# Attention and a three-stage mixer on one core: the third batch's k^T v and attention recorded earlier, the fourth batch's k, v and q asked for later

## The chip, the cores and the metric

The kernel runs on one core of one Trainium2 chip. The metric is device time in microseconds (us), the median of several executions. Engines are named as in the profile: PE is TensorE's matmul, PEld its weight load, DVE is VectorE, ACT is ScalarE, POOL is GpSimd, SP is SyncE. SP computes nothing here: it issues most of the DMAs, one after the other, and an instruction of SP that waits holds up every DMA behind it.

## The reference

For each of 8 batches (8 heads, 576 positions, head size 64, model size 512), in float32:

```python
kv  = einsum('bhsd,bhse->bhde', k, v)            # k^T v, 64 x 64 per head
out = einsum('bhsd,bhde->bhse', q, kv)
out = out / sqrt(mean(out * out, -1) + 1e-6) * g_norm
x   = out, heads side by side                    # (8, 576, 512)

theta = x @ w_theta                              # mixer, stage 1
y = w_tok_r @ (x * cos(theta)) + w_tok_i @ (x * sin(theta))
u = x + y
x = u + relu(u @ w_ch)

h = relu(x^T @ w_tok1) @ w_tok2                  # stage 2, over positions
u = x + h^T
return u + relu(u @ w_ch1) @ w_ch2               # stage 3, over channels
```

## The kernel before

Batches are numbered 0 to 7, so the third is batch 2 and the fourth is batch 3. A name in a row such as `xt24` is tile xt of batch 2, position tile 4. The 576 positions are cut into four tiles of 128 and a last one of 64, which is tile 4.

Float32 factors are split into a high and a low float16 part, so a product is three matmuls (helper `mm3`, lines 105 to 107). One batch passes through these units:

- `kv(o, part)`, unit K: k^T v into the PSUM tile kvp. Part 0 takes k and v tiles 0 and 1, part 1 takes 2, 3 and 4 (the last two have 96 rows each). Then ACT and DVE copy kvp into `kvbd` (lines 414, 415). There are three buffers each for k and v, so tiles 3 and 4 are asked for only when part 0 has read tiles 0 and 1.
- `attend(o, r)`, "a" and "n" in the recording tables: tile r of q times kvbd into PSUM (po, line 429); ACT squares (442), DVE sums (444), POOL takes a power (445, 446), DVE scales (x, 449); ACT and DVE split x into xs (465, 467); SP has a DMA transpose it into xt (468).
- `rotate(o, r)`, "r": theta = x @ w_theta (pt; line 105, or 532 for batch 0), then sine and cosine on ACT and DVE (541 to 560; 581 to 618 for tile 4) into zh and zl. Tile 4 ends with a DMA transpose from zt to zh (623).
- `residual(o, r)`, "s": x, turned, into R.
- `mix`, unit M (py), and for batch 1 `outer` (pa, pb): the two w_tok products. `channel`, unit C (pr): u @ w_ch, evicted by DVE (716), split (717, 724) and turned by a DMA transpose (728) in pairs. `token1`, unit H (ph), and `token2`, unit T (pu, evicted at 759): stage 2.
- Spare units "w" (`stash`): weights of stage 3 are loaded (wa_r), worked over on ACT, DVE and POOL (160 to 170, 335 to 345) and stored (wad), one batch of them beside each batch of the main work.

PE, DVE, ACT, POOL and SP each take their instructions in a fixed order. It comes from the order in which the code records the units, from `placed`, `lead` and `keep_in_program_order`, which tie instructions of one engine in the order of recording, and from a scheduler that orders the rest when the program is built. A recorded unit runs in steps: each next unit advances all that are pending.

`run(units, o, nxt, after, also)` records units of one batch; `also` says what is recorded beside each of them, for batch `nxt` (a, r, s) or batch `after` (n and unit K). `load_heads(b)` asks for k and v tiles 0 to 2 and for q of batch b. There is one q buffer, so q of batch 3 can only be asked for when batch 2's last attend tile has been read.

The change lies where batch 1 is in the main loop (`b == 1`), with batch 0's units H and T left over from before and batch 2's front work recorded beside them. Of what stands there before, the tables say:

```python
run(["K00"] + TOKEN1 + ["K10"] + TOKEN2, before, None, nxt, {"T00": "n0", "T02": "n1", "T10": "n2 w", "T12": "n3"})
run(CHANNEL[:1], o, nxt, None, {"C00": "a4 l"})
```

Batch 2's K units stand on both sides of batch 0's unit H, its x tiles 0 to 3 beside batch 0's unit T, its x tile 4 and the loads of batch 3 ("l") beside the first unit C of batch 1, and batch 3's K units in the middle of batch 1's units C and H.

Of the kernel before, what the change touches and what calls it, by code (L numbers as in the profile page):

```python
# [28 lines left out]
def attn_mixer_kernel(  # L29
# [175 lines left out]
    def theta_split(j):  # L205

        hi = stg.tile([P, 2 * DM], F16, tag="val", name=f"wt{j}h", bufs=2)[:, :DM]
        nc.scalar.activation(hi, wt[:, j], AF.Copy, scale=gt)
        yield
        nc.vector.scalar_tensor_tensor(wtl[:, j], wt[:, j], gt, hi, ALU.mult, ALU.subtract)  # L210
        yield
        nc.scalar.activation(wth[:, j], hi, AF.Copy)
# [138 lines left out]
    def stash_wide(g, k):  # L351
        return stash(w_ch1, f"wa{g}{k}_", k * P, g * P, [t[:, g, k] for t in wad])

    def stash_narrow(g, m):
        return stash(w_ch2, f"wb{g}{m}_", g * P, m * P, [t[:, g, m] for t in wbd])
# [12 lines left out]
    def load_kv(o, r):  # L368
        b, n = o.b, ROWS[r + 1] - ROWS[r]

        pool, bufs = (kp, 2) if b < 2 and r > 2 else (fp, 3)
        for t, src in (("k", k), ("v", v)):
            dst = pool.tile([P, DM], F32, tag=t, name=f"{t}{b}{r}", bufs=bufs)[:n]
            ins = nc.sync.dma_start(dst, src[b, ROWS[r]:ROWS[r + 1], :])
            if b == 2 and r < 3:
                tc.keep_in_program_order(ins)
            o.kv.append(dst)

    def load_heads(b):
        o = Batch()  # L380
        o.b, o.zh = b, None
        o.kv = []
        for r in range(NR + 1 if b < 2 else 3):
            load_kv(o, r)
        o.q = fp.tile([P, HP, SM + P], F32, tag="q", name=f"q{b}", bufs=1)
        qs = qT[b].rearrange("h p s -> p h s")
        if b == 0:
            nc.sync.dma_start(o.q[:, :, :P], qs[:, :, :P])
        else:
            load_q(o, 0)  # L390
        return o

    def load_q(o, at):
        qs = qT[o.b].rearrange("h p s -> p h s")
        for dst, src in ((slice(at, S), slice(at, S)), (slice(S, None), slice(SM, S))):
            ins = nc.sync.dma_start(o.q[:, :, dst], qs[:, :, src])
            if o.b == 2:
                tc.keep_in_program_order(ins)

    def kv(o, part):  # L400
# [546 lines left out]
    def go(unit, lead=False):  # L947
        advance()
        next(unit)
        (leading if lead else pending).append(unit)  # L950

    def advance():

        for units in (leading, pending):
            for g in list(units):
                try:
                    next(g)
                except StopIteration:
                    units.remove(g)

    def flush():
        while pending or leading:
            advance()
# [3 lines left out]
    def spare(n=1):  # L967
        for _ in range(min(n, len(extra))):
            go(extra.pop(0))

    def front(unit, o, r):
        if o is not None:
            go(unit(o, r))

    tk, cp, first = [], [], iter(())
    for j in range(KD):
        if j == KD - 1:
            o = load_heads(0)
        go(theta_weight(j))
# [6 lines left out]
    nxt = load_heads(1)  # L986
# [18 lines left out]
    MIX, CHANNEL, TOKEN2 = ([f"{k}{c}{i}" for c in range(2) for i in range(KD)] for k in "MCT")  # L1005
    TOKEN1 = [f"H{c}{i}" for c in range(2) for i in range(KJ)]
    UNITS = {"M": mix, "C": channel, "H": token1, "T": token2}

    def run(units, o, nxt, after, also):

        for u in units:
            kind, c, i = u[0], int(u[1]), int(u[2])
            if kind == "K":
                front(kv, after, c)
            else:
                go(UNITS[kind](o, c, i), True)
            for what in also.get(u, "").split():
                if what == "w":
                    spare()
                elif what == "l":  # L1020
                    if o.b + 2 < B:
                        loaded.append(load_heads(o.b + 2))
                elif what[0] == "a":
                    front(attend, nxt, int(what[1]))
                elif what[0] == "n":
                    front(attend, after, int(what[1]))
                elif what[0] == "r":
                    front(rotate, nxt, int(what[1]))
                elif what[0] == "s":
                    front(residual, nxt, int(what[1]))  # L1030
                elif what == "f":
                    next(first, None)
# [3 lines left out]
    STEADY = MIX[:6] + CHANNEL[:2] + MIX[6:] + CHANNEL[2:4] + ["K00"] + CHANNEL[4:] + TOKENS1[1:] + TOKEN2  # L1036
# [4 lines left out]
    for b in range(B):  # L1041
        loaded.clear()
        if b == 0:
            splits = [theta_split(j) for j in range(KD)]
            for what in "t t t t M2 r0 M3 r1 r4 . l X0 r2 X1 . r3 w X4 w w X2 w s0 s1 s2 s3 X3 .".split():
                if what == ".":
                    advance()
                elif what == "t":
                    go(splits.pop(0))
                elif what == "w":  # L1050
                    spare()
                elif what == "l":
                    loaded.append(load_heads(2))
                elif what[0] == "M":
                    go(mix(o, 1, int(what[1])), True)
                else:
                    go({"r": rotate, "X": outer, "s": residual}[what[0]](nxt, int(what[1])))
            spare(len(extra))
            flush()
            start_ctx.close()  # L1060
            wp.append(stash_ctx.enter_context(tc.tile_pool(name="wp", bufs=2, side="right", reuse_waits="tile")))
            tk.append(tok_ctx.enter_context(tc.tile_pool(name="tk", bufs=1, side="left", reuse_waits="tile")))
            extra += token_weights()
            spare(3)
            advance()
            run(CHANNEL, o, nxt, None, {"C00": "w", "C02": "w"})
            after = loaded[0]
            spare(len(extra))
            extra += [stash_wide(g, k) for g in range(KH) for k in range(DH)]
            extra += [stash_narrow(g, m) for g in range(KH) for m in range(MH)]  # L1070
            before = o
        elif b == 1:
            go(mixed(o))
            run(MIX[6:], o, nxt, None, {})
            run(["K00"] + TOKEN1 + ["K10"] + TOKEN2, before, None, nxt, {"T00": "n0", "T02": "n1", "T10": "n2 w", "T12": "n3"})
            run(CHANNEL[:1], o, nxt, None, {"C00": "a4 l"})
            after = loaded[0]
            run([u for u in STEADY[STEADY.index("C01"):] if u[0] != "M"], o, nxt, after, {
                "C01": "r0", "C02": "r1", "C10": "r2 w", "C11": "r4 s0", "C12": "s1", "H00": "s2", "H01": "r3 w s3", "H11": "n0", "T01": "n1 w", "T12": "w",
            })  # L1080
        elif b + 2 < B:
            at = STEADY.index("M02") + 1
            run(STEADY[:at], o, nxt, None, BESIDE)
            after = loaded[0]
            run(STEADY[at:], o, nxt, after, BESIDE)
        elif b + 2 == B:
            run(MIX[:6] + CHANNEL[:2] + MIX[6:] + CHANNEL[2:], o, nxt, None, {
                "M00": "a2 w", "M01": "a3", "M02": "a4 r0", "M03": "r1", "M10": "r2", "M11": "r3", "C00": "w", "M12": "r4",
            })

            spare(len(extra))
            flush()
            before, after = o, None
            stash_ctx.close()
            front_ctx.close()
            cw = ctx.enter_context(tc.tile_pool(name="cw", bufs=1, side="right", reuse_waits="tile"))
            wa = pair([P, KH, DH, 7, P], "wa", cw)
            for g in range(KH):
                for i in range(2):
                    nc.sync.dma_start(wa[i][:, g], wad[i][:, g])  # L1100
            first = chunks(0)
            ck = next(first)
        else:
            run(MIX[:6], o, None, None, {"M00": "f", "M01": "f", "M02": "f", "M03": "f"})
            run(TOKEN1, before, None, None, {})
            run(CHANNEL[:2] + MIX[6:], o, None, None, {})
            run(TOKEN2[:4], before, None, None, {})
            run(CHANNEL[2:] + TOKEN1[:2], o, None, None, {})
            run(TOKEN2[4:], before, None, None, {})
            run(TOKEN1[2:] + TOKEN2, o, None, None, {})  # L1110
        o, nxt = nxt, after
# [52 lines left out]
```

## Time and profile before

| | us |
|---|---|
| median of 3 runs | 1094.99 |
| lowest and highest run | 1094.35, 1098.6 |
| the profiled execution, its device time | 1095.65 |
| its span, first to last instruction | 1093.6 |
| PE busy in the span | 1064.7 (97%) |
| DVE busy | 807.4 (74%) |
| ACT busy | 564.9 (52%) |
| POOL busy | 184.4 (17%) |

The span is the time between the first and the last instruction of the profiled execution; its device time is 2.05 us longer. Times in rows are counted from the start of the span. Idle time of an engine that nobody waits for costs nothing.

### The profile page before, as it was taken

To read this page: it belongs to the slowest core of one execution; us is meant where nothing else is said; L and a number is where in the kernel's file an instruction comes from. 1 tells how busy PE (TensorE), PEld (TensorE's weight loads), DVE (VectorE), ACT (ScalarE), POOL (GpSimd) and SP (SyncE) were. 2 spreads that over 40 slices of the span, in tenths; PEclk is the share of its full clock that TensorE was granted. 3 is DMA by queue.
4 is the path that set the end of the run, shared out by engine and by line. 5 is a ranking of instruction groups with operands and counts; after the bars stand their busy time and mean duration, and the time that the engine had idled before them with its cause. 6 is when DMAs were issued, how large, how long until landed. Compare 5 with 4: busy or idle time off the path is not lost.

```text
span 1093.6 us, 21467 instructions
## 1 busy us (share of the span) xinstructions
PE 1064.7 (97%) x8856; PEld 812.1 (74%) x8856; DVE 807.4 (74%) x1430; ACT 564.9 (52%) x950; POOL 184.4 (17%) x255
## 2 busy tenths in 40 slices
PE   4999998999999999999999999999999999999998
PEld 3676775876768667776876777777777777777776
DVE  3999977887888878987564775858486775758484
ACT  2877547465565554656331645445363644446360
POOL 2331041533614526252000000000000000000000
DMA  9918378738858487452547301020201102020101
GB/s 304 295 21 228 71 211 194 230 81 242 205 118 241 117 222 203 119 163 51 150 169 228 124 28 60 12 77 7 82 1 44 45 23 66 12 77 1 45 1 44
DMA packets 145122, 126.05 MB, mean 115 GB/s; under 512 B 91968, under 2 KB 121792, under 8 KB 145024
## 3 DMA queue, kind: packets, MB, share of 16 engines
q1 hardware_dynamic: 139584, 104.23, 35.2%
q0 software_dynamic: 5440, 20.45, 5.2%
q8 instruction: 69, 1.13, 0.5%
q14 instruction: 29, 0.24, 0.1%
HBM read 74.25 MB, written 29.88 MB: 95 GB/s over the span
## 4 chain that ended last, share of the span: by engine, by line
PE 72%; DVE 11%; DMA 8%; ACT 4%; SPq 2%; POOL 2%; issue 1%; ACTq 0%; DVEq 0%; POOLq 0%
PE pa L105 5%; PE pa L107 5%; PE pa L106 5%; PE na L105 4%; PE na L107 4%; PE na L106 4%; DMA xt<-xs 3%; PE py L105 3%; PE py L106 3%; PE py L107 3%; PE pc L107 2%; PE pc L106 2%; PE pc L105 2%; PE nc L105 2%; PE nc L106 2%; PE nc L107 2%
## 5 line engine op out<-in xcount | busy, mean ns | idle before, releaser
L105 PE MATMUL py<-wmh,zh 128*128 128x320 f16 (+1 forms) x468 | 134.2, 287 | 1.1 <-DVE x L449 0.8
L106 PE MATMUL py<-wml,zh 128*128 128x320 f16 (+1 forms) x468 | 134.2, 287 | 0.0
L107 PE MATMUL py<-wmh,zl 128*128 128x320 f16 (+1 forms) x416 | 119.3, 287 | 0.0
L107 PE MATMUL na<-gh,wbl 128*128 128x288 f16 x384 | 109.3, 286 | 0.0
L106 PE MATMUL pa<-o,wah 128*128 128x288 f16 x384 | 109.2, 286 | 0.0
L106 PE MATMUL na<-gl,wbh 128*128 128x288 f16 x384 | 109.1, 286 | 0.0
L105 PE MATMUL pa<-o,wah 128*128 128x288 f16 x384 | 108.4, 286 | 0.0
L107 PE MATMUL pa<-o,wal 128*128 128x288 f16 x384 | 107.8, 286 | 0.0
L105 PE MATMUL na<-gh,wbh 128*128 128x288 f16 x384 | 106.0, 286 | 0.2
L832 DVE TENSOR_TENSOR gl<-sum,gh 128x1152 f16<-128x1152 f32 x48 | 65.0, 1354 | 21.9 <-ACT gh L831 21.9
L106 PEld LDWEIGHTS <-wbh 128*128 128x128 f16 x672 | 65.7, 98 | 17.8 <-issue 1.0
L105 PEld LDWEIGHTS <-wah 128*128 128x128 f16 x672 | 65.8, 98 | 16.6
L107 PEld LDWEIGHTS <-wal 128*128 128x128 f16 x672 | 65.8, 98 | 16.6
L106 PEld LDWEIGHTS <-wah 128*128 128x128 f16 x672 | 65.8, 98 | 16.6
L107 PEld LDWEIGHTS <-wbl 128*128 128x128 f16 x672 | 65.7, 98 | 16.6
L105 PEld LDWEIGHTS <-wbh 128*128 128x128 f16 x672 | 65.7, 98 | 16.6
L106 PE MATMUL pr<-ul,wch 128*128 128x256 f16 (+1 forms) x256 | 73.0, 286 | 0.0
L105 PE MATMUL pr<-uh,wch 128*128 128x256 f16 (+1 forms) x256 | 72.9, 286 | 0.0
L107 PE MATMUL pr<-uh,wcl 128*128 128x256 f16 (+1 forms) x256 | 72.6, 286 | 0.0
L105 PEld LDWEIGHTS <-zh 128*128 128x128 f16 x576 | 56.4, 98 | 17.8 <-ACT zh L557 1.2
L831 ACT ACTIVATE gh<-sum 128x1152 f16<-128x1152 f32 x48 | 55.5, 1157 | 25.6 <-DVE sum L879 25.6
L446 POOL TENSOR_TENSOR ri<-ss,mhalf 128x8 f32<-128x8 f32 x40 | 68.1, 1702 | 2.6
(293 smaller groups left out, 2915.6 us busy)
## 6 DMA issues: line engine op xcount, KB each, us to landing
c<-u2d SPq DMA_DIRECT2D x32, 288.0 KB, 4.3
out<-c SPq DMA_DIRECT2D x64, 144.0 KB, 1.8
q<-in_q SPq DMA_DIRECT2D x7, 1152.0 KB, 6.1
k<-in_k SPq DMA_DIRECT2D x24, 256.0 KB, 5.1
v<-in_v SPq DMA_DIRECT2D x24, 256.0 KB, 5.3
wa_r<-in_w_ch SPq DMA_DIRECT2D x24, 256.0 KB, 4.4
wb_r<-in_w_ch SPq DMA_DIRECT2D x24, 256.0 KB, 4.6
wad<-wa POOLq DMA_DIRECT2D x24, 224.0 KB, 4.1
```

What stands on the lines that cost most here:

```text
L105: nc.tensor.matmul(acc, ah, bh, start=first and i == 0, stop=False, **more)
L106: nc.tensor.matmul(acc, ah, bl, start=False, stop=False, **more)
L107: nc.tensor.matmul(acc, al, bh, start=False, stop=last and i == n - 1, **more)
L446: nc.gpsimd.tensor_tensor(ri, ss, mhalf, ALU.pow)
L831: nc.scalar.activation(h.hi[:, 3:], h.s, AF.Copy)
L832: nc.vector.tensor_tensor(h.lo[:, 3:], h.s, h.hi[:, 3:], ALU.subtract)
```

## The change

At the end of batch 0's part, both K units of batch 2 are recorded among batch 0's units C. Batch 2's x tiles 0 to 3 are recorded beside the last M unit and batch 0's H and T units, tile 4 ("a4") beside C01 instead of C00. Batch 3's k and v are asked for ("l") at C11, in a fixed order on SP, and its q apart from them ("q") at H10. Batch 3's K units stand between and behind batch 1's units H, and its first attend tiles later in unit T.

```diff
-            if b == 2 and r < 3:
+            if b == 2 and r < 3 or b == 3:
                 tc.keep_in_program_order(ins)
...
         if b == 0:
             nc.sync.dma_start(o.q[:, :, :P], qs[:, :, :P])
-        else:
+        elif b != 3:
             load_q(o, 0)
...
-            if o.b == 2:
+            if o.b in (2, 3):
                 tc.keep_in_program_order(ins)
...
+                elif what == "q":
+                    load_q(after, 0)
...
-            run(CHANNEL, o, nxt, None, {"C00": "w", "C02": "w"})
             after = loaded[0]
+            run(CHANNEL[:4] + ["K00"] + CHANNEL[4:7] + ["K10"] + CHANNEL[7:], o, nxt, after, {"C00": "w", "C02": "w"})
...
             go(mixed(o))
-            run(MIX[6:], o, nxt, None, {})
-            run(["K00"] + TOKEN1 + ["K10"] + TOKEN2, before, None, nxt, {"T00": "n0", "T02": "n1", "T10": "n2 w", "T12": "n3"})
-            run(CHANNEL[:1], o, nxt, None, {"C00": "a4 l"})
+            run(MIX[6:], o, nxt, None, {"M13": "a0"})
+            run(TOKEN1 + TOKEN2, before, nxt, None, {"H01": "a1", "H11": "a2", "T01": "a3", "T10": "w", "T11": "r0"})
+            run(CHANNEL[:1], o, nxt, None, {"C00": "r1"})
+            run(CHANNEL[1:6], o, nxt, None, {"C01": "a4 r2", "C10": "w", "C11": "s0 l"})
             after = loaded[0]
-            run([u for u in STEADY[STEADY.index("C01"):] if u[0] != "M"], o, nxt, after, {
-                "C01": "r0", "C02": "r1", "C10": "r2 w", "C11": "r4 s0", "C12": "s1", "H00": "s2", "H01": "r3 w s3", "H11": "n0", "T01": "n1 w", "T12": "w",
+            run(CHANNEL[6:] + ["H00", "H01", "K00", "H10", "H11", "K10"] + TOKEN2, o, nxt, after, {
+                "C12": "r4 s1", "H00": "s2", "H01": "r3 w s3", "H10": "q", "T10": "n0", "T11": "w", "T12": "n1 w",
             })
```

What this makes of the engines' orders is shown at two places.

The first place is x tile 4 of batch 2, while batch 1's units C are on PE (pr102 is unit C02, pr110 to pr113 are C10 to C13). On DVE, before, from the eviction of pr102 to xs24, the last step before tile 4 is turned:

```order
L716 SCALAR_TENSOR_TENSOR R1_608<-pr102_1836,R1_608 128x256
L545 SCALAR_TENSOR_TENSOR cs20_1825<-cs20_1825,pt20_1812 128x512
L449 TENSOR_TENSOR x24_1765<-po24_1757,ri24_1763 128x512
L724 SCALAR_TENSOR_TENSOR xs102_1835<-R1_608,xs102_1835 128x256
L716 SCALAR_TENSOR_TENSOR R1_608<-pr103_1873,R1_608 128x256
L545 SCALAR_TENSOR_TENSOR cs21_1866<-cs21_1866,pt21_1853 128x512
L553 TENSOR_TENSOR cs20_1825<-cs20_1825,x20_1620 128x1024
L467 TENSOR_TENSOR xs24_1764<-x24_1765,xs24_1764 128x512
```

On DVE now, the last twelve up to xs24; ahead of them stand the eviction of pr102 and the L545 of cs22:

```order
L553 TENSOR_TENSOR cs21_1796<-cs21_1796,x21_1606 128x1024
L724 SCALAR_TENSOR_TENSOR xs102_1862<-R1_608,xs102_1862 128x256
L716 SCALAR_TENSOR_TENSOR R1_608<-pr103_1880,R1_608 128x256
L449 TENSOR_TENSOR x24_1831<-po24_1823,ri24_1829 128x512
L716 SCALAR_TENSOR_TENSOR R1_608<-pr110_1906,R1_608 128x320
L560 TENSOR_TENSOR zl2_1729<-cs21_1796,zh2_1728 128x2x512
L724 SCALAR_TENSOR_TENSOR xs102_1862<-R1_608,xs102_1862 128x256
L716 SCALAR_TENSOR_TENSOR R1_608<-pr111_1934,R1_608 128x320
L345 SCALAR_TENSOR_TENSOR wa00_1_1897<-wa00_s_1799,wa00_0_1896 128x896
L724 SCALAR_TENSOR_TENSOR xs110_1905<-R1_608,xs110_1905 128x256
L724 SCALAR_TENSOR_TENSOR xs110_1905<-R1_608,xs110_1905 128x64
L467 TENSOR_TENSOR xs24_1830<-x24_1831,xs24_1830 128x512
```

Seven rows stood from pr102's eviction to xs24, now thirteen, with the evictions of pr110 and pr111 among them. On PE, the first matmuls that read xt24 (pt24) stood behind part of batch 3's k^T v before:

```order
L106 MATMUL pr111_1973<-ul11_1442,wch_101 128x320
L107 LDWEIGHTS wcl_102
L107 MATMUL pr111_1973<-uh11_1441,wcl_102 128x320
L409 MATMUL kvp3_1895<-v32_1777,k32_1775 64x64 x8
L409 MATMUL kvp3_1895<-v33_1921,k33_1919 64x64
L105 LDWEIGHTS wt_98
L105 MATMUL pt24_1991<-xt24_1766,wt_98 128x64
```

and stand behind pr112 now:

```order
L106 MATMUL pr112_1971<-ul11_1493,wch_101 128x320
L107 LDWEIGHTS wcl_102
L107 MATMUL pr112_1971<-uh11_1492,wcl_102 128x320
L105 LDWEIGHTS wt_98
L105 MATMUL pt24_1987<-xt24_1832,wt_98 128x64
```

From pr102 to pt24 PE now has pr103, pr110, pr111 and pr112, and no k^T v.

The second place is batch 3's first attend tile, po30. On SP, before, q of batch 3 was asked for among the transposes of batch 2's x tiles, and k and v tiles 3 and 4 behind it:

```order
L396 DMA q3_1779<-in_q 128x4x576
L396 DMA q3_1779<-in_q 128x4x64
L468 DMA_TRANSPOSE xt22_1685<-xs22_1683 128x8x128
L728 DMA_TRANSPOSE xt10_1740<-xs100_1741 128x8x128
L468 DMA_TRANSPOSE xt23_1724<-xs23_1722 128x8x128
L374 DMA k33_1919<-in_k 96x512
L374 DMA v33_1921<-in_v 96x512
```

On SP now it is the last of a row that begins at batch 1's last channel transpose and holds zh2, which is batch 2's tile 4 after its rotation:

```order
L728 DMA_TRANSPOSE xt11_1904<-xs112_1970 128x10x128
L144 DMA wa10_r_2113<-in_w_ch1 128x2x256 x2
L623 DMA_TRANSPOSE zh2_1728<-zt2_2037 128x8x128
L374 DMA k33_2145<-in_k 96x512
L374 DMA v33_2147<-in_v 96x512
L374 DMA k34_2149<-in_k 96x512
L374 DMA v34_2151<-in_v 96x512
L396 DMA q3_1965<-in_q 128x4x576
L396 DMA q3_1965<-in_q 128x4x64
```

q moved behind zh2 and behind the four loads of k and v. On PE, po30 stood behind the second half of batch 1's unit H before (ph11), with pu100 next:

```order
L746 MATMUL ph11_2097<-xt11_1927,w1rh_105 128x512
L747 LDWEIGHTS w1rl_106
L747 MATMUL ph11_2097<-xt11_1927,w1rl_106 128x512
L429 MATMUL po30_2206<-kvbd_96,q3_1779 128x128 x4
L105 LDWEIGHTS hh1_2098
L105 MATMUL pu100_2217<-w2h_107,hh1_2098 128x256
```

and now stands straight behind the last matmuls of batch 3's k^T v, which come behind pu100 to pu110:

```order
L107 MATMUL pu103_2238<-w2h_107,hl1_2068 128x256
L107 LDWEIGHTS hl1_2068
L107 MATMUL pu110_2246<-w2h_107,hl1_2068 128x320
L409 MATMUL kvp3_2127<-v34_2151,k34_2149 64x64 x8
L429 MATMUL po30_2255<-kvbd_96,q3_1965 128x128 x4
L105 LDWEIGHTS hh1_2067
L105 MATMUL pu111_2270<-w2h_107,hh1_2067 128x320
```

The copies of kvp3 into kvbd, which po30 reads, had the whole of the second half of unit H beside them before; now nothing stands between on PE.

## Rows read from the trace of the kernel before

**Rows 1.** The page: busy us, share of the span, instructions of each engine.

```profile
PE 1064.7 (97%) x8856; PEld 812.1 (74%) x8856; DVE 807.4 (74%) x1430; ACT 564.9 (52%) x950; POOL 184.4 (17%) x255
```

**Rows 2.** Timeline, PE's long waits, 120 to 345 us: start, us, [idle before].

```profile
175.76 0.20 PE L105 MATMUL pt<-xt,wt 128*128 128x64 f16 x1 [3.26 <-DMA xt<-xs]
...
188.76 0.39 PE L742 MATMUL ph<-xt,w1h 128*128 128x512 f16 x1 [1.91 <-DMA xt<-xs]
...
199.27 0.30 PE L105 MATMUL pu<-w2h,hh 128*128 128x320 f16 x1 [0.85 <-DVE R L759]
```

**Rows 3.** Timeline, PE: first matmuls of pr110 and of pt22 behind it.

```profile
165.75 0.31 PE L105 MATMUL pr<-uh,wch 128*128 128x320 f16 x1
...
167.39 0.38 PE L105 MATMUL pt<-wt,xt 128*128 128x512 f16 x1
```

**Rows 4.** Timeline, DVE, 164 to 173 us.

```profile
164.78 0.42 DVE L716 SCALAR_TENSOR_TENSOR R<-pr,R 128x256 f32<-128x256 f32 x1 [1.50 <-PE pr L107]
165.12 0.68 DVE L545 SCALAR_TENSOR_TENSOR cs<-cs,pt 128x512 f32<-128x512 f32 x1
...
167.34 0.69 DVE L467 TENSOR_TENSOR xs<-x,xs 128x512 f16<-128x512 f32 x1 [0.41 <-ACT xs L465]
...
168.48 1.09 DVE L345 SCALAR_TENSOR_TENSOR wa<-wa_s,wa 128x896 f16<-128x896 f32 x1
169.49 0.49 DVE L716 SCALAR_TENSOR_TENSOR R<-pr,R 128x320 f32<-128x320 f32 x1
169.95 1.23 DVE L560 TENSOR_TENSOR zl<-cs,zh 128x1024 f16<-128x1024 f32 x1
171.22 1.23 DVE L553 TENSOR_TENSOR cs<-cs,x 128x1024 f32<-128x1024 f32 x1
172.37 0.55 DVE L724 SCALAR_TENSOR_TENSOR xs<-R,xs 128x256 f16<-128x256 f32 x2
```

**Rows 5.** Chain of waits: two x transposes, from issue to landing.

```profile
169.84 5.87 DMA xt<-xs
...
344.55 5.04 DMA xt<-xs
```

**Rows 6.** Issue to landing: all xt transposes; q's large loads; all q loads.

```profile
DMA to landing us min/median/max: 3.0/3.4/9.0
...
q<-in_q SPq DMA_DIRECT2D x7, 1152.0 KB, 6.1
...
DMA to landing us min/median/max: 5.6/7.5/10.5
```

**Rows 7.** Timeline, PE: unit K twice, po30, first matmuls of pu100 and of pu111.

```profile
10.69 1.12 PE L409 MATMUL kvp<-v,k 128*64 128x64 f32 x16 [10.69 <-DMA v<-in_v]
...
164.67 1.15 PE L409 MATMUL kvp<-v,k 128*64 128x64 f32 x32
...
192.22 1.05 PE L429 MATMUL po<-kvbd,q 128*128 128x128 f32 x8
193.12 0.27 PE L105 MATMUL pu<-w2h,hh 128*128 128x256 f16 x1
...
197.44 0.30 PE L105 MATMUL pu<-w2h,hh 128*128 128x320 f16 x1
```

**Rows 8.** Timeline, all engines: the steps ahead of zh2, SP's issues, kvbd, unit T's evictions.

```profile
143.88 0.43 DVE L415 COPY kvbd<-kvp 64x256 f32<-64x256 f32 x1 [0.48 <-ACT kvbd L414]
...
186.19 0.58 ACT L541 ACTIVATE cs<-pt 128x512 f32<-128x512 f32 x1
...
187.43 0.69 DVE L618 TENSOR_TENSOR zt<-cs,zt 128x512 f16<-128x512 f32 x1
187.44 0.43 SPq L374 DMA_DIRECT2D v<-in_v  x1
...
188.44 1.24 SPq L623 DMA_TRANSPOSE zh<-zt  x1
...
198.80 1.81 DVE L759 SCALAR_TENSOR_TENSOR R<-pu,R 128x256 f32<-128x256 f32 x5
```

## The prediction, as it stood before the result

> **What bounds the kernel now.** The first view is the busy time of each engine on the page: PE is busy 97% of the span, DVE 74% [rows 1]. The change neither adds nor removes a matmul, a vector operation or a byte of DMA; it only moves them. So it can change the time in one way: by the moments at which PE waits, and the second view is PE's timeline over the part that is recorded differently, 120 to 345 us, read for the idle time ahead of each row. There are three waits that count: 3.26 us at pt24, for the transposed x tile xt24; 1.91 us at the second half of unit H, for a turned channel tile; 0.85 us at pu112, for DVE to evict an earlier pu from the bank that it takes [rows 2]. Together that is 6.02 us. If all three went and nothing replaced them, the time would fall by 0.55%, and that is the most that this change can bring. Some 0.5%, or 5.5 us, is about what a measurement of this kernel can tell from no change. So I look for what takes the place of these waits, and for that I read the order of the changed kernel at PE's new places and put durations of the trace on it.
>
> **First place: pt24 waits longer.** Before, pt24 stood behind pr111 and a piece of k^T v. Now it stands behind pr112, which looks later, but tile 4's attention and its split have moved back by more. I take the end of pr102 on PE as zero.
>
> On PE, pr103, pr110, pr111 and pr112 lie between that and pt24. A pr of 320 columns takes 1.64 us (165.75 to 167.39, [rows 3]); pr103 has 256 columns, 1.64 x 256/320 = 1.31. PE reaches pt24 at 1.31 + 3 x 1.64 = 6.23.
>
> On DVE, pr102's eviction can begin 0.11 after that end (my allowance for the handover), and thirteen steps run from it through xs24, in the order shown above. Steps start about 0.08 us before the one ahead has ended (164.78 + 0.42 against the next start at 165.12, [rows 4]), so each counts its duration less 0.08: two evictions of 256 columns 2 x 0.34, two of 320 columns 2 x 0.41, two of L545 or its like (L449, taken at the same size) 2 x 0.60, L553 and L560 2 x 1.15, two single L724 2 x 0.34, L345 1.01, the last two L724 together 0.47, and L467 at its full 0.69 [rows 4]. The sum is 0.68 + 0.82 + 1.20 + 2.30 + 0.68 + 1.01 + 0.47 + 0.69 = 7.85. PE finishes pr111 at 4.59 and DVE reaches its eviction at 5.4, so DVE never waits there: it is DVE's own queue that sets xs24, at 7.96.
>
> Then comes the DMA transpose. The chain shows one from issue to landing at 5.87 us, and one at 5.04 with loads and stores beside it; over all of them the least is 3.0 and the median 3.4 [rows 5, 6]. I take 5.04, because at this place the stores of the spare units and SP's other transposes run beside it, too. So xt24 is there at 7.96 + 5.04 = 13.0 and PE waits 13.0 - 6.23 = **6.8 us**; with 3.0 it waits 4.8, with 5.87 7.6. There is a floor: by the order, xs24 cannot come before the eviction of pr111, so even an idle DVE leaves 0.11 + 0.41 + 1.01 + 0.47 + 0.69 + 3.0 - 1.64 = 4.1. The old 3.26 does not go away; it grows.
>
> **Second place: po30 gets a wait.** Before, the copies of k^T v into kvbd and the arrival of q were hidden behind half of unit H. Now nothing stands between kvp3's last part and po30. Zero here is the end of pt23.
>
> q's issue sits on SP behind zh2's transpose and four loads. zh2 needs zt2, and L618, which makes it, stands on DVE behind L545 of pt23. So: ACT's L541 0.58, DVE's L545 0.68, L618 0.69 and some 0.15 of handovers make 2.1; the transpose holds SP 1.24, say 1.3; four issues of 0.43 with gaps are 1.8 [rows 4, 8]. q is issued at 5.2 and its large load lands 6.1 later [rows 6], at 11.3. On PE, K00 takes 1.08 (164.67 to 165.75, [rows 3, 7]), the second half of unit H 3.46 (188.76 to 192.22), unit T up to pu110 4.32 (193.12 to 197.44) less an attend tile that stood in it, 0.90 as po30 (192.22 to 193.12), so 3.42, and K10, with three tiles for K00's two, 1.62 [rows 2, 7]. That is 9.6, so PE waits **1.7 us** for q. If q landed early there would still be kvbd: it stands on DVE behind five evictions (1.81) and takes 0.43 itself [rows 8], while PE has only the unit's four last matmuls and the last eight of kvp3, about 1.1, beside them; with handovers a floor of 1.35. If q takes the 10.5 of the slowest q load [rows 6], the wait is 6.1.
>
> **What goes.** At the second half of unit H, the unit pt23 and K00 now stand between the last channel product and the first matmul that reads the turned tile: about 6.3 us of PE's work against 4.9 of eviction, split, issue and landing at 3.4, 6.5 at 5.04. I take the 1.91 as gone, with 0.2 left at worst. pu112 now follows po30's wait, in which DVE catches up on its evictions: 0.85 gone, or at worst all still there. The rest I cost at nothing: batch 2's k^T v at the end of batch 0 has its loads well ahead (if the cover fails, about 1 us at tile 4's v); pt20 has a margin of some 0.6 us over its transpose (at 5.87 instead, a wait near 1 us); K10 needs loads issued four SP slots before q, and any wait there comes off the wait at po30.
>
> **Sum.** 6.8 + 1.7 - 6.02 = +2.5 us on the profiled 1095.65, so 1098.15. The profiled execution was 0.66 above the median of its runs, so the median is **1097.5**.
>
> **A rule against the change.** What the rows show: sixteen matmuls of kvp that follow PE's first wait, of 10.69 us, take 1.12, while thirty-two of the same kind take 1.15 later on, which is half the pace; and pt24's matmuls behind 3.26 us were not slowed [rows 2, 7]. A wait of 6.8 lies between. The Trainium skill, "TensorE: Matmul & The Clock Gate", section "HAM oscillation — how this bites in real kernels", says that waits for data between groups of matmuls can drop TensorE's clock to half, so that the next group starts slow; by it the matmuls behind the longer wait would cost more, where the row at 3.26 gives nothing. It is a rival below, priced from rows.
>
> **Rivals and chances.**
> - *As forecast*, waits of about 6.8 and 1.7: 1096 to 1099.3. Chance 0.45.
> - *Both waits near their floors.* The median transpose lands in 3.4, and no row shows that this one must be slow: 4.8 + 1.35 - 6.02 = +0.1, so 1095; with the floor of 4.1, 1094.4. Against it: two transposes in the chain took over 5. Chance 0.25.
> - *A slow pace behind pt24's wait.* The two rows leave it open; price from nothing to one pr's matmuls at half pace, 1.64 more: up to 1099.2. It needs the wait to be nearer 10.69 than 3.26 in its effect. Chance 0.12.
> - *The other side, slower: q lands late.* It has a megabyte and is behind four loads that it shares the queue with; at 10.5 the sum is 6.8 + 6.1 - 6.02 = +6.9, so 1101.9. It decides from a landing of about 9.1 on. Against it: the seven large q loads have 6.1. Chance 0.13.
> - *The change does what it says and more*: tile 4 is not late because DVE reorders less than I think, and PE's waits go: down to 1089 to 1093. The orders of the engines are fixed, so this needs a wrong reading of mine. That batch 2's x is done sooner holds for tiles 0 to 3; tile 4, which alone was waited for, now stands behind pr101. Chance 0.05.
>
> The range reaches from just above the last case into the late q: 1093.5 to 1102. Faster by over 0.5% (under 1089.5) 0.03, slower (over 1100.5) 0.17, and within 0.5% 0.80.
>
> **What would show it.** In PE's timeline of the changed kernel: the wait at pt24, released by the DMA of xt24, at 4.8 to 7.6 and with xs24 on DVE about 1.7 after PE is free; no wait ahead of the second half of unit H and at pu112; a new wait at po30 straight behind kvp3's last eight, with the DMA of q as its releaser (if it is DVE's kvbd, and near 1.35, q was early); the pace of the matmuls that follow pt24's wait. The prediction is wrong if pt24 waits under 4, if po30 does not wait, or if a wait over 1 us appears at a place that I cost at nothing, pt20 and batch 2's k^T v above all.

## The result: slower by 0.63%, and the profile after

| | before | after |
|---|---|---|
| median, us | 1094.75 | 1102.41 |
| lowest and highest of 6 runs | 1094.35, 1098.6 | 1101.3, 1104.53 |
| the profiled execution, its device time | 1095.65 | 1101.67 |
| its span | 1093.6 | 1099.7 |
| mean granted TensorE clock over the span | 1.000 | 0.994 |

The ratio, estimated from all runs of both kernels and not from the two medians, is 1.0063 (95% interval 1.0045 to 1.0080). Forecast was 1097.5 with a range up to 1102: the sign of the likeliest case was right, its size was not, and the median lies 0.4 us above the end of the range.

The page of the changed kernel, busy us by engine, and the granted clock in 40 slices (tenths of full speed, 9 is 90% or more; a slice is 27.5 us):

```profile
PE 1069.0 (97%) x8856; PEld 815.0 (74%) x8856; DVE 808.4 (74%) x1430; ACT 565.3 (51%) x950; POOL 183.7 (17%) x255
...
PEclk9999998999999999999999999999999999999999
```

PE does the same 8856 matmuls as before [rows 1], yet is busy 4.3 us longer, and one slice, that from 165 to 192 us, has a lower clock. A busy time that grows with the same instructions says that some of them ran slower. PE's timeline shows where it waits (the four rows in which something of the change is late, and the second attend tile behind them):

```profile
177.19 0.23 PE L105 MATMUL pt<-xt,wt 128*128 128x64 f16 x1 [7.16 <-DMA xt<-xs]
...
196.99 0.69 PE L409 MATMUL kvp<-v,k 96*64 96x64 f32 x16 [0.56 <-DMA v<-in_v]
...
199.10 0.69 PE L409 MATMUL kvp<-v,k 96*64 96x64 f32 x16 [0.75 <-DMA v<-in_v]
...
202.03 1.13 PE L429 MATMUL po<-kvbd,q 128*128 128x128 f32 x8 [2.24 <-DVE wa_s L169]
...
205.93 1.41 PE L429 MATMUL po<-kvbd,q 128*128 128x128 f32 x8
```

The waits at the second half of unit H and at pu112 [rows 2] are gone, pt24's has grown from 3.26 to 7.16, and around po30 there are three new ones, 3.55 us in all. The releaser named at 202.03, a stash row on DVE, is only the one whose end lies nearest: it writes nothing that po30 reads. SP's timeline has q's issue, two loads from 193.89 on, and the list of DMA issues of that stretch the time from issue to landing of the large one, 8.0 us, so it is there at 201.9:

```profile
193.89 1.24 SPq L396 DMA_DIRECT2D q<-in_q  x2
```

```profile
q<-in_q SPq DMA_DIRECT2D x1, 1152.0 KB, 8.0
```

DVE's timeline from pr102's eviction, the first row, to xs24, the last, and the chain of waits behind it:

```profile
163.87 0.42 DVE L716 SCALAR_TENSOR_TENSOR R<-pr,R 128x256 f32<-128x256 f32 x1 [0.17 <-PE pr L107]
...
166.88 0.67 DVE L449 TENSOR_TENSOR x<-po,ri 128x512 f32<-128x512 f32 x1
...
169.34 0.48 DVE L716 SCALAR_TENSOR_TENSOR R<-pr,R 128x320 f32<-128x320 f32 x1
169.74 1.08 DVE L345 SCALAR_TENSOR_TENSOR wa<-wa_s,wa 128x896 f16<-128x896 f32 x1
170.74 0.55 DVE L724 SCALAR_TENSOR_TENSOR xs<-R,xs 128x256 f16<-128x256 f32 x2
171.21 0.68 DVE L467 TENSOR_TENSOR xs<-x,xs 128x512 f16<-128x512 f32 x1
```

```profile
172.12 5.03 DMA xt<-xs
...
190.53 1.24 SPq L623
...
193.38 5.58 DMA v<-in_v
```

From the eviction's start to xs24's end is 8.02, against 7.85 forecast, with no gap in which DVE waits, and the transpose takes 5.03 for the 5.04 taken. In the second half of the chain, zh2's transpose and the load of v of tile 4 follow one another on SP, and kvp3 on PE waits for that load.

The granted clock by stretches (the columns are us, busy time and count of PE, PEld, DVE, ACT, POOL, then the clock, the DMA share, which can read over 1 in this view, and GB/s):

```profile
165.00:172.00 7.00, 5.03 (x38) 3.40 (x35) 7.00 (x13) 5.79 (x10) 3.97 (x7) 1.00 0.33 78
172.00:178.00 6.00, 0.81 (x16) 0.81 (x17) 5.28 (x10) 2.56 (x4) 0.00 (x0) 0.54 1.08 248
178.00:182.00 4.00, 4.00 (x46) 3.08 (x44) 0.47 (x2) 0.38 (x1) 0.00 (x0) 0.50 0.95 328
182.00:186.00 4.00, 4.00 (x20) 1.94 (x19) 2.41 (x7) 2.42 (x5) 0.00 (x0) 0.90 0.16 56
186.00:202.00 16.00, 12.47 (x137) 7.76 (x135) 11.83 (x21) 8.12 (x15) 4.35 (x7) 1.00 0.94 245
202.00:204.00 2.00, 1.97 (x13) 1.63 (x14) 0.84 (x2) 0.60 (x1) 1.25 (x3) 0.81 1.08 371
204.00:206.00 2.00, 2.00 (x10) 1.24 (x8) 1.00 (x2) 0.00 (x0) 1.43 (x4) 0.50 1.07 408
206.00:208.00 2.00, 2.00 (x16) 1.76 (x16) 0.49 (x1) 0.62 (x2) 0.83 (x1) 0.83 1.01 380
```

The clock falls from 2.4 to 1.2 GHz during pt24's wait and stays there when PE works again, to some 182.8 us. It falls a second time at about 203.2, some 1.2 us after the wait at po30 has ended. These two stretches are the 4.3 us of longer busy time: behind pt24's wait its 48 matmuls take 2.56 us for 1.41 before, and pr113 3.10 for 1.63, which is 2.6; the other 1.7 lie behind po30. In the profile of before, the clock held through pt24's wait, though the DMA engines were as busy:

```profile
172.00:176.00 4.00, 0.74 (x24) 0.60 (x21) 1.52 (x4) 0.21 (x2) 0.00 (x0) 1.00 1.13 297
```

One more difference between the two profiled executions has nothing to do with the change. The same matmul, with the same wait ahead of it, comes 1.76 us earlier in the second, since the very first loads landed sooner; of before, then of after:

```profile
91.08 0.28 PE L105 MATMUL pa<-wmh,zh 128*128 128x256 f16 x1 [1.12 <-ACT zh L557]
```

```profile
89.32 0.28 PE L105 MATMUL pa<-wmh,zh 128*128 128x256 f16 x1 [1.12 <-ACT zh L557]
```

So the account from profile to profile is: +3.90 at pt24, +3.55 around po30, -2.76 for the two waits that went, +4.3 for the slow clock, -1.76 at the start, and some -1 of small waits, most of them in later batches that PE, being late, no longer meets. That is +6.2; the spans differ by 6.1. Without the start it is about 8, and the medians differ by 7.7.

### The profile page after: what moved, and what is told of

Read it like the earlier page. It is cut to its first block, busy times and chain, and to the rows that moved or that the text cites. A ratio compares the mean times of both kernels' runs of the same rounds, so it can differ in the third digit from the quotient of the medians.

```text
span 1099.7 us, 21472 instructions
## 1 busy us (share of the span) xinstructions
PE 1069.0 (97%) x8856; PEld 815.0 (74%) x8856; DVE 808.4 (74%) x1430; ACT 565.3 (51%) x950; POOL 183.7 (17%) x255
## 4 chain that ended last, share of the span: by engine, by line
PE 87%; DVE 6%; DMA 3%; ACT 2%; issue 1%; POOL 1%; SPq 0%; DVEq 0%; POOLq 0%; ACTq 0%
PE py L105 5%; PE py L106 5%; PE py L107 5%; PE pa L105 5%; PE pa L107 5%; PE pa L106 5%; PE na L105 4%; PE na L107 4%; PE na L106 4%; PE po L429 3%; PE pr L105 2%; PE pr L106 2%; PE pr L107 2%; PE pt L105 2%; PE pt L106 2%; PE pt L107 2%
```

## The experiments

Theory after the result: the loss has two places, pt24 and po30, and at each the wait is paid twice, once as a wait and once as a slow clock behind it. Rivals: the clock falls for another reason, such as the load on the DMA engines (its share is over 0.9 in both places); or one part of the change is harmless by itself.

### 1. PE kept busy during pt24's wait

```diff
+            for i in range(28):
+                tc.keep_in_program_order(nc.tensor.matmul(ptb, wth[:, i % KD, :P], wth[:, i % KD, :], start=True, stop=True))
```

The matmuls go into pt24's own PSUM bank, which its first matmul overwrites, and are tied so that the order around them stays as in the changed kernel.

> The changed kernel, with 28 matmuls of 128x512 (some 6.1 us) added on PE ahead of pt24; they compute nothing that is kept. xt24 still comes as late, so pt24 starts no sooner. Theory (the clock falls because PE stands still for 7.16 us): PE is busy through most of the wait, the clock stays at 1.00 there, pt24 to pr113 run at full pace and the kernel gains what the slow stretch cost, some 2.5 us: about 1099.9 against 1102.4. Rival (the clock falls there for a reason other than the wait, such as the load on the DMA engines): the granted clock falls to 0.5 all the same and the time stays at 1102.4.

Measured 1099.62 (five runs from 1099.14 to 1101.6, the changed kernel's six from 1101.3 to 1104.53), a ratio of 1.0042 (1.0029 to 1.0055) to before. The edit moves the line numbers of the rows by three. In PE's timeline pt24 starts as late as it did (0.75 later, in an execution that is 0.96 later already at the matmul of 89.32), behind what is left of the wait, and q is now the releaser named at po30:

```profile
177.94 0.19 PE L108 MATMUL pt<-xt,wt 128*128 128x64 f16 x1 [0.91 <-DMA xt<-xs]
...
199.94 2.05 PE L432 MATMUL po<-kvbd,q 128*128 128x128 f32 x8 [2.38 <-DMA q<-in_q]
```

The same stretches as above, and that behind po30's wait:

```profile
172.00:178.00 6.00, 5.09 (x27) 2.22 (x25) 5.86 (x12) 3.03 (x6) 0.54 (x1) 1.00 1.04 253
178.00:182.00 4.00, 4.00 (x65) 3.00 (x65) 1.34 (x3) 1.03 (x3) 0.00 (x0) 1.00 1.00 283
199.00:203.00 4.00, 3.06 (x13) 2.56 (x14) 1.72 (x3) 0.60 (x1) 1.27 (x3) 0.57 1.09 362
```

The DMA engines are as busy as before (1.04 against 1.08), the wait for xt24 is as long, and the clock stays at 1.00: PE's standing still brings it down, not the transfers. Adding 28 matmuls made the kernel 2.8 us faster by the medians. That is the price of the first slow stretch, 2.6 by the rows above. At po30, where nothing was filled, the clock still falls.

### 2. q sooner

```diff
             after = loaded[0]
+            load_q(after, 0)
...
-"H01": "r3 w s3", "H10": "q", "T10": "n0"
+"H01": "r3 w s3", "T10": "n0"
```

> The changed kernel, with q of batch 3 asked for right behind the six loads of k and v tiles 0 to 2, some 14 us sooner. Theory: po30 waited for q; now it waits only for kvbd, about 1.3 us for 2.24, and the four loads of k and v no longer share the queue with q, so the 0.56 and 0.75 at kvp3 shrink; with less standing still the second slow stretch goes too. Gain 0.9 + 1 + 1.8: about 1099. Rival (the wait at po30 is DVE's, behind the stash rows): it stays at 2.2 and the time at 1102.4. Rival (q's megabyte delays the transposes ahead of unit H): a wait at ph11 or pt23 over 1 us, and no gain.

Measured 1099.52 (1.0037, 1.0023 to 1.0050). PE's waits:

```profile
177.22 0.23 PE L105 MATMUL pt<-xt,wt 128*128 128x64 f16 x1 [7.06 <-DMA xt<-xs]
...
189.62 0.39 PE L742 MATMUL ph<-xt,w1h 128*128 128x512 f16 x1 [1.37 <-DMA xt<-xs]
...
200.02 1.16 PE L429 MATMUL po<-kvbd,q 128*128 128x128 f32 x8 [1.28 <-DVE kvbd L415]
```

```profile
188.00:203.00 15.00, 12.35 (x128) 8.54 (x123) 11.14 (x19) 7.20 (x12) 3.72 (x8) 1.00 0.99 306
```

The wait at po30 becomes kvbd's, 1.28 (the floor of the prediction was 1.35), those at kvp3 go, and the clock holds there. The third case came true in part: q now stands ahead of a channel transpose, and 1.37 comes back at the second half of unit H. 3.55 - 1.28 - 1.37 = 0.9 of waits, and the gain is 2.9, so the second slow stretch cost about 2 (1.7 by the rows). Here no matmuls were added: that the shorter waits are what holds the clock is argued from this experiment; the DMA share is 0.99 in this stretch with the clock at 1.00.

### 3 and 4. x tile 4 sooner, alone and with q sooner

```diff
-{"H01": "a1", "H11": "a2", "T01": "a3", "T10": "w", "T11": "r0"}
+{"H01": "a1", "H11": "a2", "T01": "a3", "T10": "w", "T11": "a4 r0"}
...
-"C01": "a4 r2"
+"C01": "r2"
```

> The changed kernel, with x tile 4 of batch 2 recorded beside T11, ahead of r0, and not beside C01: xs24 stands on DVE ahead of pr102's eviction and not twelve rows behind it. Theory: the wait of 7.16 at pt24 goes, and with it the slow stretch behind it, 9.5 us together: about 1093 against 1102.4, with the waits around po30 and the second slow stretch still there. Rival (the slow stretch isn't the wait's): only 7.2 us are gained, and the clock still falls near 175 us: 1095.2. Rival (tile 4's steps push the steps of tiles 0 to 3 back by as much): waits at pt22, pt23 or the pr units appear and less than 5 us are gained.

Measured 1092.96 (0.9981, 0.9972 to 0.9990), 9.45 below the changed kernel where 9.5 was forecast. PE does not wait at pt24; what it waits for now:

```profile
183.21 0.44 PE L742 MATMUL ph<-xt,w1h 128*128 128x512 f16 x1 [2.48 <-DMA xt<-xs]
...
194.57 1.16 PE L429 MATMUL po<-kvbd,q 128*128 128x128 f32 x8 [1.28 <-DVE kvbd L415]
```

```profile
183.00:187.00 4.00, 3.79 (x10) 1.39 (x11) 0.00 (x0) 0.38 (x2) 1.22 (x3) 0.57 0.86 212
```

pt24's wait and its slow stretch went as expected, but that the total agrees to 0.05 is luck. Around po30, where all was expected to stay, the waits fell from 3.55 to 1.28 and the slow stretch went; about as much came back at the second half of unit H, a wait of 2.48 and a slow stretch behind it.

With the q of the second experiment added:

> The two edits together: x tile 4 beside T11, q behind the k and v loads. Theory: 9.5 of the one and 3.5 of the other, less what the two have in common: about 1090, which is faster than before by 0.4%. Rival: with PE some 9 us sooner, k and v tiles 3 and 4 or q are late again and the second group of waits comes back: 1093 or more.

Measured 1095.94 (1.0000, 0.9991 to 1.0009), the rival's side and worse than tile 4 alone. With 0.62 and 0.66 at kvp3, the most is lost at a place that neither named:

```profile
184.62 0.61 PE L742 MATMUL ph<-xt,w1h 128*128 128x512 f16 x1 [4.86 <-DMA xt<-xs]
```

In SP's timeline six loads of k and v and the large part of q stand ahead of the two last channel transposes, whose issues last until 182.54. By the chain of waits the second transpose has landed 6.10 after its issue at 178.48; in the third experiment, without q ahead of it, 5.22 after 177.94. PE also comes there 0.97 sooner than in the third. That the loads make the transpose slow is how I read it, and the sixth experiment bears on it.

```profile
173.28 0.43 SPq L374 DMA_DIRECT2D v<-in_v  x1
173.81 0.38 SPq L396 DMA_DIRECT2D q<-in_q  x1
174.29 8.25 SPq L728 DMA_TRANSPOSE xt<-xs  x2
```

### 5, 6 and 7. k and v sooner, then q, then the K units

All three have x tile 4 beside T11. In the fifth, `l` moves from C11 to C00; in the sixth q is asked for at C01 as well; in the seventh batch 3's K units move too:

```diff
-{"C00": "r1"} ... "C11": "s0 l"
+{"C00": "l r1"} ... "C11": "s0"
...
-"C01": "r2" ... "H10": "q", "T10": "n0"
+"C01": "q r2" ... "T10": "n0"
...
-run(CHANNEL[6:] + ["H00", "H01", "K00", "H10", "H11", "K10"] + TOKEN2, ...
+run(CHANNEL[6:] + ["K00", "H00", "H01", "K10", "H10", "H11"] + TOKEN2, ...
```

> The kernel with x tile 4 beside T11, and batch 3's k and v asked for beside C00 and not C11; q stays at H10. With x tile 4 sooner alone, PE waited 2.48 at the second half of unit H for a turned channel tile, whose two transposes stood on SP behind the six loads of k and v, and the clock fell behind it. Theory: the loads held these transposes up; now the wait is under 0.9 and the slow stretch goes, some 3.5 us in all: about 1089.5 against 1092.96. Rival (the transposes are slow by themselves, as xt24's 5.04): the wait stays over 2 and the time at 1093. Rival (PE, now sooner, meets q at po30): 1.5 us or more there, and half of the gain lost.

Measured 1097.33 (1.0011, 0.9998 to 1.0024): slower than without the move. PE does meet q at po30, but less because PE is sooner (192.52 for 193.29) than because q is 2.6 later: zh2's transpose, ahead of it on SP, is issued at 183.96 for 182.64, and q takes 8.5 to land for 7.2. The waits are 0.66 and 1.42 at the two halves of unit H, 1.35 at kvp3, and

```profile
195.90 2.05 PE L429 MATMUL po<-kvbd,q 128*128 128x128 f32 x8 [3.38 <-DMA q<-in_q]
```

> As the one with k and v beside C00, and q beside C01 too, ahead of all transposes of channel tiles. Theory: what cost 4.86 at the second half of unit H when both edits were made was that ten loads stood ahead of the transposes, not q being sooner; here q has landed before them. No wait for q or at kvp3; kvbd stays at 1.3: about 1089. Rival (q's megabyte costs the transposes their bandwidth wherever it stands): a wait over 1 us at ph10 or pt24, 1091 or more.

Measured 1092.73 (0.9971, 0.9959 to 0.9982), 4.6 below the fifth and 3.7 above what was expected, on the rival's side: there is a wait of 1.83 at the first half of unit H (ph10), 1.32 at kvp3, and 0.93 at po30 behind it, where the clock falls to 0.50. The second half of unit H no longer waits. q, asked for at 164.43, took 9.0 to land, so it had not landed ahead of the channel transposes, which begin at 166.12.

> As the one before, and batch 3's K units moved up: part 0 behind C13, part 1 behind H01, so that kvp3's last part is ahead of unit T and po30 behind its first tiles. Theory: the 1.28 at po30 (kvbd, behind five evictions, with nothing of PE beside it) is hidden by unit T, and the k^T v between the last channel product and unit H covers its transposes: about 1087.5 to 1088, no wait over 0.5 between 120 and 345 us. Rival (k and v tiles 3 and 4 are asked for behind part 0, and are late for part 1 at its new place): a wait of 1 to 3 at kvp3, 1089 to 1091.

Measured 1091.60 (0.9954, 0.9940 to 0.9969), with a mean clock of 1.000 in each of its five runs. Between 120 and 245 us only one wait over 0.5 us is left, 0.58 at ph10. The expectation of 1088 was missed because two waits of 1.37 and 1.73 appear later, in the next batch's unit H (at 247 and 255 us). Why they appear was not tried.

### 8 and 9. Each half of the change by itself

```diff
-run(CHANNEL[1:6], o, nxt, None, {"C01": "a4 r2", "C10": "w", "C11": "s0 l"})
+run(CHANNEL[1:2], o, nxt, None, {"C01": "a4 l r2"})
...
-run(CHANNEL[6:] + ["H00", "H01", "K00", "H10", "H11", "K10"] + TOKEN2, o, nxt, after, {
+run([u for u in STEADY[STEADY.index("C02"):] if u[0] != "M"], o, nxt, after, {
```

This is the eighth; its q is asked for in `load_heads` again. It records batch 2 as in the change, and batch 3's loads, q and K units as before, the loads behind tile 4 at C01. The ninth records batch 2 as before, but for the rotation of its tile 4, which stays beside C12 as in the change, and batch 3's loads, q and K units as in the change.

> The third batch's part of the change alone: batch 2's k^T v and x tiles recorded as changed (tile 4 beside C01), batch 3's loads with its q right behind them at C01, and its K units and first attend tile where they stood before. Theory: the loss at pt24 is this part's. From pr102's end PE reaches pt24 at 7.9 (K pieces stand between again), DVE has 7.1 to do, and with 5.0 from issue to landing PE waits some 4.3 with a slow stretch behind it; no wait over 1 at po30: 1095 to 1097, about as before, since the waits of 1.91 and 0.85 go. Rival (the later k^T v alone does the harm): pt24 waits under 2 and the kernel is faster than before by 3 us or more.

> The fourth batch's part of the change alone: batch 2 recorded as before (its tile 4 beside C00), batch 3's k and v asked for at C11, its q at H10, its K units between and behind batch 1's units H. Theory: this part's own loss is around po30: waits of 0.5 to 1 at kvp3 twice and 2.2 or more for q, with a slow stretch of some 1.8 us behind them; pt24 waits under 1, since pt21 and pt22 lie between pr102 and it: 1093 to 1094.5 against 1095.7. Rival (the loss around po30 comes only because PE was late or early by the first part): no wait over 1.3 at po30, no slow stretch, and 1091 or less.

Measured: the third batch's part alone 1092.63 (0.9976, 0.9967 to 0.9986), the fourth batch's alone 1099.47 (1.0033, 1.0021 to 1.0045). PE's waits in the first, and the granted clock behind the longer one:

```profile
176.33 0.24 PE L105 MATMUL pt<-xt,wt 128*128 128x64 f16 x1 [3.51 <-DMA xt<-xs]
...
196.11 0.30 PE L105 MATMUL pu<-w2h,hh 128*128 128x320 f16 x1 [0.53 <-DVE R L759]
```

```profile
176.00:180.00 4.00, 3.67 (x55) 3.30 (x56) 2.43 (x7) 0.80 (x2) 0.00 (x0) 0.58 1.16 264
```

The waits in the second:

```profile
191.58 0.69 PE L409 MATMUL kvp<-v,k 96*64 96x64 f32 x16 [3.27 <-DMA v<-in_v]
...
194.09 1.12 PE L409 MATMUL kvp<-v,k 96*64 96x64 f32 x16 [1.83 <-DMA v<-in_v]
...
198.40 2.04 PE L429 MATMUL po<-kvbd,q 128*128 128x128 f32 x8 [3.17 <-DMA q<-in_q]
```

The clock among them, and q in the chain of waits, from issue to landing:

```profile
193.00:198.00 5.00, 1.12 (x16) 0.97 (x16) 2.14 (x4) 0.93 (x2) 0.00 (x0) 0.50 1.04 347
198.00:203.00 5.00, 4.61 (x19) 3.42 (x20) 1.70 (x4) 1.44 (x2) 2.71 (x7) 0.50 1.07 374
```

```profile
188.82 9.44 DMA q<-in_q
```

I had put the first at 1095 to 1097 and the second at 1093 to 1094.5: both wrong, and the other way round. Batch 3's loads at their new place cost 8.3 us of waits here, with a slow clock from 193 us on, where the changed kernel had 3.55. PE comes to kvp3's third part at 188.3 (191.58 less the wait), in the changed kernel at 196.4, 8.1 later, while v of tile 3 is asked for only 5.1 later there (187.35 and 192.44); that the 7.16 lost at pt24 gave the loads time to land there is how I read it, and was not tried by itself. By the orders, the third batch's part is a gain as long as batch 3's k^T v still stands ahead of pt24 and hides part of the wait. The percentages do not add up (-0.24 and +0.33 against +0.63). At pt24 the halves wait 3.51 and not at all, against 3.26 before, and the whole 7.16, since the fourth batch's part takes that cover away; around po30 the halves have none and 8.3, and the whole 3.55. The rest of the difference, the slow clock among it, was not worked out.

### 10 and 11. The half that gains, with x tile 4 sooner

As the eighth, with tile 4 beside T11 (or beside C00) and batch 3's loads and q beside C00:

```diff
-"T10": "w", "T11": "r0" ... {"C00": "r1"} ... "C01": "a4 l r2"
+"T10": "w", "T11": "a4 r0" ... {"C00": "l r1"} ... "C01": "r2"
```

The eleventh has `"C00": "a4 l r1"` in place of both.

> The third batch's part alone with its x tile 4 sooner still: beside T11, with batch 3's loads and q beside C00; batch 3's K units and first attend tile stand where they stood before the change. Theory: with tile 4 beside C01 this part left one wait of 3.51 at pt24 and a slow stretch of some 1.7 behind it; both go, and 0.53 at pu112 stays at most: 1092.63 - 5 = about 1087.5, and no granted clock below 1. Rival (q and the loads, sooner, hold up the x and channel transposes): a wait of 1 to 2 at ph10 or the second half of unit H, 1089 to 1091.

> The same with x tile 4 and the loads beside C00, where they stood before the change. By the order xs24 stands five rows behind pr102's eviction on DVE and not ten: some 4.4 us from pr102's end, 9.4 with a landing of 5.0, against PE's 7.9: a wait of 1.5 at most where the third batch's part alone had 3.51, and no slow stretch: 1088.5 to 1089.5. Rival (the transpose of xt24 stands behind q and four loads on SP and lands later still): a wait over 3 and no gain over 1092.6.

Measured 1089.80 (0.9952, 0.9939 to 0.9965) and 1091.04 (0.9962, 0.9949 to 0.9975). The tenth has a mean clock of 1.000 in all five runs, the lowest median of all kernels here, and beats both the kernel before and the changed one. Its waits of over 0.5 us between 120 and 345 us are two. The time lies in the rival's range, and the rival's place (unit H) is the right one for what separates it from 1087.5, with a wait a little shorter than it named:

```profile
183.62 0.39 PE L742 MATMUL ph<-xt,w1h 128*128 128x512 f16 x1 [0.88 <-DMA xt<-xs]
...
193.99 0.30 PE L105 MATMUL pu<-w2h,hh 128*128 128x320 f16 x1 [0.70 <-DVE R L759]
```

The eleventh, expected at 1088.5 to 1089.5, missed that by 1.5: it waits 0.51 at pt24, as expected, but 1.23 at unit H, and the clock fell a little in three of its seven runs.

## Why the prediction was right in its sign and short in its size

**pt24 waits longer.** Right, step by step: 7.85 of DVE's queue forecast and 8.02 measured, 5.04 from issue to landing and 5.03, a wait of 6.8 and 7.16. Experiment 3 takes tile 4 out of this queue and the wait goes.

**po30 gets a wait.** The place and the releaser were right, one term was too small. q took 8.0 from issue to landing and not 6.1, and this 1.9 is the difference between 1.7 forecast and 3.55 measured. The 1.31 at kvp3, which I had costed at nothing because any wait there comes off po30's, did come off it: q's landing at 201.9 sets po30, whether PE stands still ahead of kvp3 or behind it. The floor of 1.35 for kvbd showed itself as 1.28 in experiments 2 and 3. The wrong step is taking the median of the seven large q loads for this one. The list of DMA issues of before, from 140 to 166 us, has this very load, batch 3's, which stood among transposes there and not behind four loads:

```profile
q<-in_q SPq DMA_DIRECT2D x1, 1152.0 KB, 7.9
```

With 7.9 the same working gives a wait of 3.5. In the experiments this load took from 5.7 (the eighth) to 9.8 (the eleventh); what sets that was not tried.

**What goes.** Right: nothing is left at the second half of unit H and at pu112, and no wait appears at pt20 or at batch 2's k^T v.

**The slow pace behind the waits.** This is the step that failed. It stood among the rivals with a chance of 0.12, a price of at most 1.64, at one place. It came at both places and cost 4.3 us by PE's busy time, 2.8 at the first by experiment 1 and about 2 at the second by experiment 2 (2.6 and 1.7 by the rows). Two things led me there. I took the profiled execution's 3.26 us without a slow stretch [rows 2] as the kernel's habit. In 67 of the 71 further runs of the kernel before the mean granted clock was 0.997 or 0.998, and 1.000 in 4: the profiled execution was one of a few. These runs do not say where in the span the clock fell. And I priced the stretch as one pr's matmuls where the clock stayed low for some 5.6 us after PE had begun again at 177.19, through pt24's own matmuls and pr113's. The Trainium skill's rule that I had weighed against the row ("TensorE: Matmul & The Clock Gate", section "HAM oscillation — how this bites in real kernels") speaks of groups of matmuls that start slow after a wait for data; the traces agree, at 7.16 us and, in experiments 3 and 8, behind waits of 2.48 and 3.51.

**The sum.** +2.5 forecast; with 7.16, 3.55 and 4.3 in the places of 6.8, 1.7 and nothing, the same sum gives +9, and +7.7 was measured in the medians. The kernel before has a slow stretch of its own in most runs, which the profiled one lacks; that goes the right way. The median of the 67 runs is 1095.9 and that of the 4 with a clock of 1.000 is 1093.4, so it may be some 2.4 us, by four runs only. For the same reason the agreement of 8 and 7.7 in the account above may be in part luck: one side of it has a kernel before without slow clock, the other mostly with it. The rival of a late q ends near what was measured, at 1101.9, but by a way that was not taken: it decides from a landing of 9.1 on, and q took 8.0. Two slips in the working leave the sum as it is: fourteen steps are added up for DVE where the text says thirteen, and the rival of both floors takes the wait of 4.8, which belongs to a landing of 3.0, for one of 3.4.

What stays open: how the wait and the slow stretch depend on each other in length. 3.26 us had no slow stretch in one execution, 2.48 had one in another; in experiment 2 waits of 1.37 and 1.28 had none, and in experiment 6 a wait of 1.83 had none, but 1.32 and 0.93 close behind one another had one.

## What to carry to other kernels

Where an engine is 97% busy, moving an instruction sooner is worth the wait that it removes, and the slow clock behind that wait where there is one; what it is moved past may become a wait, and a wait of PE can be paid again as a slow clock behind it. To see it, compare PE's busy time before and after with the same instructions. When a step is moved, count the rows that stand ahead of it on every in-order engine, SP's DMA issues above all: q and k loads ahead of a channel transpose, or behind a transpose that waits, decided several of these experiments. A row of the very transfer that is moved is worth more than the median of its kind: 7.9 stood in the trace of before. And test the halves of a change apart: here one half was a gain, and the other took away what hid its remaining wait.

## What the hardware showed that I had not expected

Twenty-eight more matmuls made the kernel 2.8 us faster, since they kept the clock at 1.00 through a wait of 7 us. And the same kernel ran with a mean granted clock of 0.997 to 0.998 in 67 of 71 runs and 1.000 in 4, so one profiled execution did not show what clock this kernel has as a rule.
